# Clustered attention with an MLP behind it: loading and preparing the first keys and queries side by side, and queueing what later units need behind the first units

## The chip, the cores and the metric

The kernel runs on one core of a Trainium2 chip. The time is device microseconds (us) of one execution; the number given for the kernel before is the median of 3 runs. One further execution was profiled, and all durations below come from it.

## The reference

Four batches, 8 heads, 768 positions, head size 64, 16 cluster centres per head; then an MLP from 512 over 2048 back to 512 on all 3072 rows.

```python
q_assign = argmax(q_n . c_n); k_assign = argmax(k_n . c_n)        # nearest centre, per position
scores = where(q_assign == k_assign, (q . k) / 8, -1e9)
attn = softmax(scores);  x = attn . v                             # per batch and head
h = x @ w_in;  g = s * relu(h)**2 + b;  out = g @ w_out
```

## The kernel before

**Units.** The attention is cut into 192 units (`units`): a batch b, a pair of row tiles c (3 per batch), a pair of heads hp (4), a row tile t and a head h. Unit i takes 128 query rows of one head against all 768 keys. `scores` (L446, matmuls at L454) makes a 128x768 score tile in PSUM out of four matmuls: two with the transposed tiles KA and QA, two with KB and QB. `maxima` (L463) takes the row maximum on DVE, `exps` (L470 on DVE, L473 on ACT) the exponential `p`, `high` and `low` split p into two halves of 16 bits and turn them with a transposing DMA (L498), `values` (L502 on) multiplies by v. The first eight units (`RAW`) are done otherwise: p stays in 32 bits, PE turns it (L493), DVE and ACT copy the turned halves out of PSUM (L115, L117), and v is used as loaded. Score tiles have two PSUM buffers.

**Preparation.** `prep_k(b, hp)` makes KA and KB for a pair of heads: load `kn` (L78), row maximum on DVE (L97), maximum over the partitions by PE (`am_k`, L93, L94), a power-of-two scale `ksm` (L69 to L71, L65), a high half `ka` on ACT (L175), a low half `kb` on DVE (L177), a copy (L323), two transposing DMAs (L327, L328), matmuls with the centres (`pk`, L337, L338), a one-hot code of the nearest centre on DVE (`onehot`, L284 to L290) written into kb, and kb's transpose once more (L341). KB is complete only with that last DMA. `prep_q` does the same for the queries of four heads (loads `qn`; `qsm`; ACT L170, L171; POOL L173; DMAs L378 and L391). `prep_v` loads the four tiles `vn`, takes a common scale `vm` and splits each into `vh` (ACT L175) and `vl` (DVE L177). All three are generators: each `yield` is a place where the caller can turn to another one.

**Weights.** `weights` brings in w_in and w_out as 32 tiles of 512 KB, in turn; tile number p is `wst_p`, in a ring of three staging buffers (`stage`). `rebase` (ACT L193 and L195), `narrow` (DVE L199 and L200) and `bound` (PE L211 with DVE L212, or ACT L206; then POOL L213) turn one into the 32-bit tile `wi` or `wo`. A staging buffer is free when rebase and narrow of its tile are done. Three tiles are begun ahead of the units, and then one per unit.

**What sets the order.** All work is emitted as one Python sequence, and a scheduler at build time orders each engine's queue by priority and its own clock. On the chip every engine runs its queue strictly in order. All DMAs are issued by one queue (SP). `first_of_all` raises the priority of the first 20 units. In the kernel before, keys 0 and 1 and queries 0 are prepared in full one after the other, three weight tiles are begun, and `prepare(0)` to `prepare(3)` put keys 2 and 3, queries 1 and the first batch's v between the first units. Two small loads that spread the scalars s and b over 128 partitions (`sv`, `bv`, L121) are emitted before the keys.

The eight units that follow one load of queries need keys 0 (units 0 to 3) and keys 1 (units 4 to 7). Units 8 to 15 need keys 2 and 3 and queries 1. The MLP begins 21 units behind the attention and then takes a step per unit.

Of the kernel before, what the change touches and what calls it, by code (L numbers as in the profile page):

```python
# [2 lines left out]

# [11 lines left out]
ALU = mybir.AluOpType  # L15
# [11 lines left out]
def tile_cluster_attention_mlp(ctx, tc, q, k, v, cent, w_in, w_out, s_in, b_in, out):  # L27
# [44 lines left out]


    last_transpose = [None]

    def load(dst, src, free=False):
        if last_transpose[0] is None or free:
# [41 lines left out]
    def scalar_in(src, name):  # L119
        every = const([P, 1], F32, name)  # L120
        nc.sync.dma_start(every, src.partition_broadcast(P))  # L121
        return every


    ct = sb.tile([P, 2, D], F32, tag="r", name="ct", bufs=2)
    cn = ct[:, 0, :]
# [41 lines left out]
    def split(hi, lo, src, f, early):  # L168
        if early:
            A.activation(src, src, AF.Copy, scale=f)  # L170
            A.activation(hi, src, AF.Copy)  # L171
            yield
            G.tensor_tensor(lo, src, hi, op=ALU.subtract)  # L173
        else:
            A.activation(hi, src, AF.Copy, scale=f)  # L175
            yield
            V.scalar_tensor_tensor(lo, src, f, hi, op0=ALU.mult, op1=ALU.subtract)  # L177

# [119 lines left out]
    def prep_k(b, hp):  # L298
# [21 lines left out]
        else:  # L320
            ka = sb.tile([P, 2, T, 2, D], F16, tag="big", name=f"ka_{n}", bufs=BIGN)
        yield from split(ka[:, :, :, 0, :], kb[:, :, :, 0, :], kn, sm[2], False)
        V.tensor_copy(ka[:, :, :, 1, :], ka[:, :, :, 0, :])  # L323
        KA = sb.tile([P, 2 * T, P], F16, tag="KA", name=f"KA_{n}", bufs=5)
        KB = sb.tile([P, 2 * T, P], F16, tag="KB", name=f"KB_{n}", bufs=5)
        KS[(b, hp)] = (KA, KB)
        nc.sync.dma_start_transpose(KA, ka.rearrange("p h t e d -> p (h t e d)"))  # L327
        nc.sync.dma_start_transpose(KB, kb.rearrange("p h t e d -> p (h t e d)"))  # L328
        yield
        yield  # L330
        pa = (ps_m if b or not hp else ps_h).tile([P, 512], F32, tag="m" if b or not hp else "h", name=f"pk_{n}")
# [6 lines left out]
                nc.tensor.matmul(o, KB[:, i, :], cT[:, 2, hc], start=False, stop=True)  # L338
        mk = kb.rearrange("p h t e (r c) -> p (h t) e r c", c=C)[:, :, 1, :, :]
        yield from onehot(pa, 2 * T, f"k{n}", mk, BIG, -BIG)  # L340
        nc.sync.dma_start_transpose(KB, kb.rearrange("p h t e d -> p (h t e d)"))  # L341

    def prep_q(b, c, hq):
        n = f"{b}_{c}_{hq}"
# [53 lines left out]
    def prep_v(b):  # L398
        vm = sb.tile([P, 8], F32, tag="vm", name=f"vm_{b}", bufs=2)
        VM[b] = vm  # L400
        vns = []
        for hp in range(NP):
            vn = sb.tile([P, 2, T, D], F32, tag="kv", name=f"vn_{b}_{hp}", bufs=5)
            load(vn, v[b, 2 * hp : 2 * hp + 2].rearrange("h (p t) d -> p h t d", t=T), b == 0)
            vns.append(vn)
            if b == 0:
                VN[hp] = vn
            yield
        for hp in range(NP):
            absmax(vm[:, hp : hp + 1], vns[hp].rearrange("p h t d -> p (h t d)"))  # L410
            if hp < NP - 1:
                yield
        vc = columns(1, f"v{b}")
        V.tensor_reduce(vc, vm[:, 0:NP], axis=AX.X, op=ALU.max)
        if b:
            yield
        allmax(vm[:, 5:6], vc, f"v{b}")
        yield
        floor2(V, vm[:, 6:7], vm[:, 5:6])
        inverse2(V, vm[:, 7:8], vm[:, 6:7], 0)  # L420
        V.tensor_scalar(vm[:, 7:8], vm[:, 7:8], 2.0 ** 13, None, op0=ALU.mult)
        V.tensor_scalar(vm[:, 6:7], vm[:, 6:7], 2.0 ** -19, None, op0=ALU.mult)
        for hp in range(NP):
            vh = sb.tile([P, 2, T, D + 2], F16, tag="vh", name=f"vh_{b}_{hp}", bufs=5)
            vl = sb.tile([P, 2, T, D], F16, tag="vl", name=f"vl_{b}_{hp}", bufs=5)
            VS[(b, hp)] = (vh, vl)
            G.memset(vh[:, :, :, D:], 1.0)
            yield from split(vh[:, :, :, :D], vl, vns[hp], vm[:, 7:8], False)
            if hp < NP - 1:
                yield  # L430
                if b > 0:
                    yield
                    yield
# [11 lines left out]
    def scores(i):  # L445
# [5 lines left out]
        for X, Y, st in ((QA, KA, True), (QB, KB, False)):  # L451
            y = Y.rearrange("p n q -> p (n q)")
            for e in range(2):
                nc.tensor.matmul(  # L454
                    sc[:, e, :HALF], X[:, col, :], y[:, h * S + e * HALF : h * S + (e + 1) * HALF], start=st, stop=not st
                )
        U[i] = {"sc": sc[:, :, :HALF], "scale": qs[:, 3, hp % 2 : hp % 2 + 1]}

    def maxima(i):
        j = i % 4  # L460
        if j == 0:
            SM[i // 4] = sb.tile([P, 4, 4], F32, tag="ssm", name=f"ssm_{i}", bufs=4)
        V.tensor_reduce(SM[i // 4][:, 0, j : j + 1], U[i]["sc"], axis=AX.XY, op=ALU.max, negate=True)  # L463

    def exps(i):
        j = i % 4
# [3 lines left out]
        V.tensor_scalar(bi, sm[:, 0, j : j + 1], u["scale"], LIFT, op0=ALU.mult, op1=ALU.add)  # L470
        p = sb.tile([P, S], F32, tag="big", name=f"p_{i}", bufs=BIGN)
        total = {"accum_out": sm[:, 2, j : j + 1]} if i < RAW else {}
        A.activation(p.rearrange("p (a b) -> p a b", a=2), u["sc"], AF.Exp, bias=bi, scale=u["scale"], **total)  # L473
        u["p"] = p

    turned = ps_a.tile([P, CT, DM], F32, tag="acc", name="turned")
# [170 lines left out]
            nc.sync.dma_start(out[b * S : (b + 1) * S].rearrange("(p t) e -> p t e", t=T)[:, c * CT : (c + 1) * CT, :], o)  # L647


    sv = scalar_in(s_in, "sv")  # L650
    bv = scalar_in(b_in, "bv")
    steps = [(b, c, ft) for b in range(B) for c in range(NCH) for ft in range(NF)]
    NS = len(steps)
    active = []
# [29 lines left out]
    def run(gen):  # L684
        for _ in gen:
            pass

    def prepare(k):
        if k == 0:
            run(prep_k(0, 2))  # L690
            run(prep_k(0, 3))
            run(prep_q(0, 0, 1))
        if k == 1:
            for _ in range(5):
                next(first_v)
        if k == 3:
            next(first_v)
            next(first_v)
            active.append(first_v)

    first_v = prep_v(0)
    run(prep_k(0, 0))
    run(prep_k(0, 1))
    run(prep_q(0, 0, 0))
    for _ in range(3):
        next(wgen, None)
    i = 0
    while i < NU + 8 or i - LAG < NS + 4:
        m = i - LAG
# [61 lines left out]
```

## Time and profile before

| | |
|---|---|
| median of 3 runs | 1036.81 us (1032.09, 1036.81, 1037.48) |
| the profiled execution, whole | 1039.74 us |
| its span from first to last instruction | 1037.7 us |
| busy share of PE, DVE, ACT, POOL | 82%, 67%, 65%, 51% |
| mean busy share of the DMA queue's 16 engines | 75% |

The profile's page has five parts that matter here: busy time by engine, the span in 40 slices, the chain of work that ended last, groups of instructions, and DMA issues. The trace behind it answers by time: the instructions of one engine in order, with the idle time ahead of each and what ended it, or the busy time of every engine in chosen stretches. PE is the matmul engine, PEld its weight loads, DVE the vector engine, ACT the scalar engine, SPq the issue of DMAs by the SP queue. "PEclk" is the granted share of PE's clock. L12 is line 12 of the kernel before.

### The profile page before, as it was taken

The page shows a single profiled execution, that of the slowest core. Times are in us where ns is not written, and L with a number is a line of the kernel's source. Part 1 is how long each engine was busy: PE and PEld are TensorE (multiplying, and loading weights), DVE is VectorE, ACT ScalarE, POOL GpSimd, SP SyncE. Part 2 cuts the span into 40 slices and gives each one's busy share as a digit, 9 for nine tenths or more (in the row PEclk, how much of TensorE's full clock was granted, in tenths as well). Part 3 has the DMA queues.
Part 4 walks back from the last instruction along what each step waited for, and adds up shares of the span by engine and source line. Part 5 has one row for each costly group of instructions (what it writes and reads, how often), then busy time and mean ns, then how long its engine had stood idle before and what let it go on. Part 6 is the DMA issues. An engine that isn't in the chain of part 4 may idle for free.

```text
span 1037.7 us, 22320 instructions
## 1 busy us (share of the span) xinstructions
PE 855.8 (82%) x8536; PEld 588.5 (57%) x8536; DVE 692.8 (67%) x1690; ACT 679.5 (65%) x1232; POOL 527.7 (51%) x502
## 2 busy tenths in 40 slices
PE   0137766788888999988889898987788899999997
PEld 0125544555555677655557675655556676667764
DVE  6568688798798666777778755568767557674210
ACT  3136667668778778765668676655576677777543
POOL 2104465554467756554457565544455556666422
PEclk9998568999999999999889999999999899999999
DMA  8645689997687868799888978779896678877500
GB/s 237 155 91 143 154 208 209 201 218 139 128 154 138 153 117 138 149 196 156 183 159 154 168 126 160 142 136 197 154 171 118 142 124 163 136 125 134 81 27 21
DMA packets 473339, 153.16 MB, mean 148 GB/s; under 512 B 440976, under 2 KB 469648, under 8 KB 473232
## 3 DMA queue, kind: packets, MB, share of 16 engines
q1 hardware_dynamic: 473232, 151.73, 75.2%
q8 instruction: 67, 1.10, 0.4%
q14 instruction: 40, 0.33, 0.1%
HBM read 35.69 MB, written 6.29 MB: 40 GB/s over the span
## 4 chain that ended last, share of the span: by engine, by line
PE 40%; DVE 20%; DMA 14%; issue 6%; ACT 5%; POOL 4%; SPq 3%; POOLq 0%; DVEq 0%; ACTq 0%
PE h L591 14%; PE acc L635 13%; PE sc L454 6%; DVE ssm L463 4%; DMA kn<-in_k_dram 3%; POOL ph L496 3%; DMA KB<-kb 2%; DMA QB<-qb 2%; PE px L515 2%; DVE qa L177 2%; DMA wst<-in_moe_w_in_dram 2%; PE px L517 2%; PE px L516 2%; DMA qn<-in_q_dram 1%; ACT ph L483 1%
## 5 line engine op out<-in xcount | busy, mean ns | idle before, releaser
L496 POOL TENSOR_TENSOR ph<-p,ph 128x768 f16<-128x768 f32 x184 | 308.5, 1677 | 244.5 <-ACT ph L483 181.8
L635 PE MATMUL acc<-wos,g 128*128 128x512 f16 x1056 | 275.9, 383 | 6.0 <-POOL g L620 4.1
L591 PE MATMUL h<-x,wis 128*128 128x256 f16 x2112 | 269.3, 277 | 10.5 <-DMA x<-xn 6.2
L591 PEld LDWEIGHTS <-wis 128*128 128x128 f16 x2112 | 207.1, 99 | 63.8 <-issue 15.5
L473 ACT ACTIVATE p<-sc,ssm,qsm 128x768 f32<-128x768 f32 x192 | 188.2, 980 | 56.9 <-DVE ssm L470 30.5
L463 DVE TENSOR_REDUCE ssm<-sc 128x1 f32<-128x768 f32 x192 | 181.2, 950 | 50.0 <-PE sc L454 49.8
L620 POOL TENSOR_TENSOR g<-r,g 128x256 f16<-128x256 f32 x176 | 125.2, 713 | 111.2 <-ACT r L608 102.8
L483 ACT ACTIVATE ph<-p 128x768 f16<-128x768 f32 x184 | 153.3, 833 | 26.2 <-DMA PT<-ph 21.2
L601 ACT ACTIVATE r<-h,cf 128x256 f32<-128x256 f32 x176 | 82.2, 467 | 110.8 <-PE h L591 90.3
L515 PE MATMUL px<-vh,PT 128*128 128x65 f16 x1104 | 124.1, 199 | 23.7 <-DVE xs L529 7.1
L635 PEld LDWEIGHTS <-g 128*128 128x128 f16 x1056 | 95.2, 98 | 81.6 <-POOL g L620 7.9
L454 PE MATMUL sc<-KA,QA 128*128 128x384 f16 x384 | 101.0, 345 | 29.6 <-ACT p L473 17.4
L516 PE MATMUL px<-vl,PT 128*128 128x64 f16 x1104 | 124.4, 196 | 0.0
L517 PE MATMUL px<-vh,PT 128*128 128x65 f16 x1104 | 124.2, 197 | 0.0
L515 PEld LDWEIGHTS <-PT 128*128 128x128 f16 x1104 | 106.0, 100 | 29.3 <-issue 21.6
L516 PEld LDWEIGHTS <-PT 128*128 128x128 f16 x1104 | 106.0, 102 | 19.0 <-issue 10.8
L454 PE MATMUL sc<-KB,QB 128*128 128x384 f16 x384 | 101.1, 346 | 13.4 <-DMA QB<-qb 13.4
L517 PEld LDWEIGHTS <-PT 128*128 128x128 f16 x1104 | 106.1, 100 | 4.6 <-issue 1.1
L607 ACT ACTIVATE g<-r 128x256 f16<-128x256 f32 x176 | 72.8, 414 | 3.5
L608 ACT ACTIVATE r<-r 128x256 f32<-128x256 f32 x176 | 72.4, 412 | 3.5
L454 PEld LDWEIGHTS <-QA 128*128 128x128 f16 x384 | 35.3, 102 | 55.5 <-issue 25.2
L454 PEld LDWEIGHTS <-QB 128*128 128x128 f16 x384 | 38.4, 102 | 45.2 <-DMA QB<-qb 17.1
(165 smaller groups left out, 1161.0 us busy)
## 6 DMA issues: line engine op xcount, KB each, us to landing
wst<-in_moe_w_in_dram SPq DMA_DIRECT2D x16, 512.0 KB, 5.1
wst<-in_moe_w_out_dram SPq DMA_DIRECT2D x16, 512.0 KB, 4.5
kn<-in_k_dram SPq DMA_DIRECT2D x16, 384.0 KB, 3.8
vn<-in_v_dram SPq DMA_DIRECT2D x16, 384.0 KB, 4.0
qn<-in_q_dram SPq DMA_DIRECT2D x24, 256.0 KB, 3.7
out_dram<-o SPq DMA_DIRECT2D x12, 512.0 KB, 3.9
PT<-ph SPq DMA_TRANSPOSE x184, 4.0
x<-xn SPq DMA_TRANSPOSE x44, 2.9
```

Source lines behind the costliest of these rows:

```text
L454: nc.tensor.matmul(sc[:, e, :HALF], X[:, col, :], y[:, h * S + e * HALF : h * S + (e + 1) * HALF], start=st, stop=not st)
L463: V.tensor_reduce(SM[i // 4][:, 0, j : j + 1], U[i]["sc"], axis=AX.XY, op=ALU.max, negate=True)
L473: A.activation(p.rearrange("p (a b) -> p a b", a=2), u["sc"], AF.Exp, bias=bi, scale=u["scale"], **total)
L483: A.activation(u["ph"][:, 0, :], u["p"], AF.Copy)
L496: G.tensor_tensor(u["ph"][:, 1, :], u["p"], u["ph"][:, 0, :], op=ALU.subtract)
L515: nc.tensor.matmul(o1, PT[:, kt, :], vh[:, h, kt, : D + 1], start=(kt == 0), stop=False)
L516: nc.tensor.matmul(o, PT[:, kt, :], vl[:, h, kt, :], start=False, stop=False)
L517: nc.tensor.matmul(o1, PT[:, T + kt, :], vh[:, h, kt, : D + 1], start=False, stop=(kt == T - 1))
L591: nc.tensor.matmul(ph[:, :CW], WSP[ft][0][:, wl, kt, :], XS[(b, c, kt)][:, :, xl, :], start=(i == 0), stop=(i == len(terms) - 1))
L601: A.activation(r, ph[:, :CW], AF.Relu, scale=MS[(b, c)][0])
L620: G.tensor_tensor(g[:, 1, :], r, g[:, 0, :], op=ALU.subtract)
L635: nc.tensor.matmul(acc[:, t, :], g[:, gl, rows], WSP[ft][1][:, wl, :], start=(ft == 0 and gl + wl == 0), stop=(ft == NF - 1 and gl == 1))
```

## The change

The loads of keys 0, queries 0, keys 1, keys 2, keys 3 and queries 1 are emitted first, in this order, before any other work on them. Keys 0, queries 0 and keys 1 then go through their preparation in small steps in turn (`some(gen, n)` takes n steps). Keys 2, keys 3 and queries 1 (`second`) are taken two steps further at once, behind the first three's splits; their transposes come behind the last transpose of the first three; their centre matmuls and one-hot codes come after units 0, 1 and 2, one of them each.

The new helper `behind` puts each instruction emitted inside it behind a named instruction of the same engine, in the order alone (it adds no wait): behind the last split on DVE and ACT, the last transposing DMA on SP, the last score matmul, maximum and exponential. The loads of v, of s and b and of the weights are now emitted behind a transposing DMA, v in single steps between units 1 to 4.

```diff
+    last_turn = [None]
+    last_split = [None, None]
+    last_score = [None]
+    last_max = [None]
+    last_exp = [None]
...
+    def behind(*last):
+        stack = ExitStack()
+        for ins in last:
+            if ins is not None:
+                stack.enter_context(tc.issue_after(ins.ins))
+        return stack
...
-            load(vn, v[b, 2 * hp : 2 * hp + 2].rearrange("h (p t) d -> p h t d", t=T), b == 0)
+            load(vn, v[b, 2 * hp : 2 * hp + 2].rearrange("h (p t) d -> p h t d", t=T), False)
...
-    sv = scalar_in(s_in, "sv")
-    bv = scalar_in(b_in, "bv")
...
     def prepare(k):
         if k == 0:
-            run(prep_k(0, 2))
-            run(prep_k(0, 3))
-            run(prep_q(0, 0, 1))
-        if k == 1:
-            for _ in range(5):
-                next(first_v)
-        if k == 3:
-            next(first_v)
-            next(first_v)
-            active.append(first_v)
+            with behind(last_transpose[0]):
+                for gen in second:
+                    next(gen)
+        with behind(last_score[0], last_exp[0], last_max[0]):
+            if k == 1:
+                run(first_k[2])
+                some(first_v, 1)
+            if k == 2:
+                run(first_k[3])
+                some(first_v, 1)
+            if k == 3:
+                run(first_q[1])
+                some(first_v, 2)
+            if k == 4:
+                some(first_v, 1)
+                active.append(first_v)
 
     first_v = prep_v(0)
-    run(prep_k(0, 0))
-    run(prep_k(0, 1))
-    run(prep_q(0, 0, 0))
-    for _ in range(3):
-        next(wgen, None)
+    first_k = [prep_k(0, hp) for hp in range(NP)]
+    first_q = [prep_q(0, 0, hq) for hq in range(2)]
+    second = [first_k[2], first_k[3], first_q[1]]
+    for gen in (first_k[0], first_q[0], first_k[1], *second):
+        next(gen)
+    some(first_k[0], 2)
+    some(first_k[1], 2)
+    some(first_q[0], 2)
+    some(first_k[0], 1)
+    some(first_q[0], 1)
+    some(first_k[1], 1)
+    with behind(*last_split):
+        for _ in range(2):
+            for gen in second:
+                next(gen)
+    with behind(last_turn[0], *last_split):
+        some(first_v, 1)
+        sv = scalar_in(s_in, "sv")
+        bv = scalar_in(b_in, "bv")
+        some(wgen, 3)
+    run(first_k[0])
+    run(first_q[0])
+    run(first_k[1])
+    last_transpose[0] = last_turn[0]
```

The other lines record the instructions that `behind` names (`last_turn` at the transposes of KB, `last_split` at the high half and at L323's copy, and so on). No operation is added or removed; the amount of work is the same. In the changed kernel line numbers are 5 to 40 higher: L93 has become L98, L121 L126, L175 L187, L193 L205, L199 L211, L290 L302, L328 L340, L341 L353, L391 L403, L463 L475, L473 L485.

## What was predicted

> **What bounds the kernel now.** I read busy time by stretches first, then the queues of ACT, DVE and SP up to 101 us. The stretches, with the columns PE, PEld, DVE, ACT, POOL busy (and instructions), PE's clock, the DMA engines' busy share, GB/s:
>
> ```profile
> span 1037.7 us, 22320 instructions
> 0.00:47.90 47.90, 5.75 (x76) 3.50 (x77) 29.32 (x89) 14.57 (x26) 8.22 (x38) 1.00 0.75 195
> 47.90:70.20 22.30, 3.22 (x54) 1.78 (x52) 14.97 (x43) 5.67 (x10) 0.14 (x1) 1.00 0.57 116
> 70.20:95.40 25.20, 20.30 (x140) 15.79 (x141) 18.76 (x43) 15.84 (x33) 9.31 (x9) 0.93 0.52 129
> 95.40:100.80 5.40, 3.47 (x20) 2.38 (x20) 5.37 (x13) 4.19 (x10) 1.16 (x1) 0.72 0.59 191
> 100.80:160.00 59.20, 37.31 (x293) 26.22 (x291) 46.86 (x95) 37.71 (x64) 32.05 (x22) 0.64 0.74 166
> 160.00:240.00 80.00, 62.63 (x550) 42.51 (x551) 65.25 (x162) 56.97 (x102) 42.19 (x31) 0.96 0.97 207
> 240.00:1038.00 798.00, 723.13 (x7413) 496.29 (x7408) 512.29 (x1250) 544.52 (x994) 434.61 (x403) 0.97 0.75 139
> ```
>
> From 240 us on PE is busy 91% of the time (723 of 798): it is the bound. From 160 to 240 the DMA engines are at 97%. In the first 70 us nothing is full: PE works 9 us in all, and from 47.9 to 70.2 ACT 5.7 of 22.3 us. What holds the units there is seen in ACT's queue:
>
> ```profile
> 44.00 0.94 ACT L175 ACTIVATE ka<-kn,ksm 128x768 f16<-128x768 f32 x1 [5.95 <-DVE ksm L71]
> 56.16 0.93 ACT L175 ACTIVATE ka<-kn,ksm 128x768 f16<-128x768 f32 x1 [11.23 <-DVE ksm L71]
> 57.01 3.40 ACT L175 ACTIVATE vh<-vn,vm 128x768 f16<-128x768 f32 x4
> 68.77 0.91 ACT L170 ACTIVATE qn<-qn,qsm 128x256 f32<-128x256 f32 x2 [8.37 <-DVE qsm L361]
> 70.19 0.97 ACT L473 ACTIVATE p<-sc,ssm,qsm 128x768 f32<-128x768 f32 x1
> ...
> 100.79 1.01 ACT L473 ACTIVATE p<-sc,ssm,qsm 128x768 f32<-128x768 f32 x1
> ```
>
> and in DVE's:
>
> ```profile
> 7.59 0.95 DVE L97 TENSOR_REDUCE amb_k<-kn 128x1 bf16<-128x768 f32 x1 [2.93 <-DMA kn<-in_k_dram]
> ...
> 23.12 0.36 DVE L284 TENSOR_REDUCE om_k<-pk 128x12 f32<-128x192 f32 x1
> ...
> 43.61 0.29 DVE L290 TENSOR_SCALAR qb<-oo_q 128x512 f16<-128x512 f16 x1
> ...
> 47.93 1.82 DVE L463 TENSOR_REDUCE ssm<-sc 128x1 f32<-128x768 f32 x2 [1.68 <-PE sc L454]
> 49.67 0.33 DVE L470 TENSOR_SCALAR ssm<-ssm,qsm 128x1 f32<-128x1 f32 x2
> ...
> 95.37 0.94 DVE L463 TENSOR_REDUCE ssm<-sc 128x1 f32<-128x768 f32 x1
> ```
>
> Units 0 and 1 have maximum and bias at 50.0, but their exponentials come at 70.2: ACT stands in front of keys 3 (idle 11.2 us), v, and queries 1 (idle 8.4 us), which units 0 to 7 don't need. The exponential at 100.79 is unit 8's, the ninth. So the first unit costs 70.2 us, the next eight 30.6, and the other 183 the rest.
>
> **The change, part by part.** *ACT's queue.* Before, from the last weight operation ahead of unit 0 (`vh` is v's high half, `p_0` unit 0's exponential):
>
> ```order
> L206 ACTIVATE wo2_578,l1_131<-wo2_578 128x512
> L175 ACTIVATE ka_2_335<-kn_0_2_324,ksm_0_0_142 128x12x64
> L175 ACTIVATE ka_3_391<-kn_0_3_380,ksm_0_0_142 128x12x64
> L175 ACTIVATE vh_0_0_644<-vn_0_0_514,vm_0_513 128x12x64
> L175 ACTIVATE vh_0_1_727<-vn_0_1_516,vm_0_513 128x12x64
> L175 ACTIVATE vh_0_2_820<-vn_0_2_518,vm_0_513 128x12x64
> L175 ACTIVATE vh_0_3_909<-vn_0_3_520,vm_0_513 128x12x64
> L170 ACTIVATE qn_0_0_1_434<-qn_0_0_1_434,qsm_0_0_1_436 128x256 x2
> L171 ACTIVATE qb_0_0_1_450<-qn_0_0_1_434 128x4x64 x2
> L473 ACTIVATE p_0_496,ssm_0_493<-sc_0_488,ssm_0_493,qsm_0_0_0_253 128x768
> ```
>
> The changed kernel, same engine, same place:
>
> ```order
> L205 ACTIVATE wi1_273<-wst_2_274 128x512
> L218 ACTIVATE wo0_265,l1_131<-wo0_265 128x512
> L207 ACTIVATE wsg_2_417<-wst_2_274 128x512
> L485 ACTIVATE p_0_402,ssm_0_399<-sc_0_394,ssm_0_399,qsm_0_0_0_177 128x768
> L485 ACTIVATE p_1_463,ssm_0_399<-sc_1_456,ssm_0_399,qsm_0_0_0_177 128x768
> L485 ACTIVATE p_2_528,ssm_0_399<-sc_2_521,ssm_0_399,qsm_0_0_0_177 128x768
> L120 ACTIVATE PT_0_465<-turned_135 128x384
> L205 ACTIVATE wo1_413<-wst_3_414 128x512
> L207 ACTIVATE wsg_3_482<-wst_3_414 128x512
> L485 ACTIVATE p_3_591,ssm_0_399<-sc_3_584,ssm_0_399,qsm_0_0_0_177 128x768
> ```
>
> Keys 2, keys 3 and queries 1 went ahead of the weights, out of unit 0's way; v's halves went behind unit 6. But weight tile 3 now stands in front of unit 3, so that unit waits for a load.
>
> *SP's queue.* Before, around the last transposes for unit 0 (KB_0 and QB_0 complete with L341 and L391):
>
> ```order
> L78 DMA wst_4_546<-in_moe_w_in_dram 128x4x256
> L341 DMA_TRANSPOSE KB_0_0_157<-kb_133 128x12x128
> L78 DMA wst_5_579<-in_moe_w_out_dram 128x1024
> L341 DMA_TRANSPOSE KB_0_1_213<-kb_1_195 128x12x128
> L378 DMA_TRANSPOSE QA_0_0_0_275<-qa_0_0_0_266 128x8x128
> L391 DMA_TRANSPOSE QB_0_0_0_276<-qb_0_0_0_267 128x8x128
> ```
>
> The changed kernel:
>
> ```order
> L340 DMA_TRANSPOSE KB_0_1_211<-kb_1_140 128x12x128
> L83 DMA vn_0_0_256<-in_v_dram 128x2x384
> L126 DMA sv_258<-in_moe_s_dram 128x1
> L126 DMA bv_260<-in_moe_b_dram 128x1
> L83 DMA wst_0_263<-in_moe_w_in_dram 128x4x256
> L83 DMA wst_1_266<-in_moe_w_out_dram 128x1024
> L83 DMA wst_2_274<-in_moe_w_in_dram 128x4x256
> L353 DMA_TRANSPOSE KB_0_0_199<-kb_133 128x12x128
> L403 DMA_TRANSPOSE QB_0_0_0_206<-qb_0_0_0_191 128x8x128
> L353 DMA_TRANSPOSE KB_0_1_211<-kb_1_140 128x12x128
> ```
>
> The scalars and three weights moved from the head of the queue to just ahead of unit 0's last transposes; after these rows come five transposes for units 8 to 15 and only then `wst_3`.
>
> *First keys.* How fast the queue moves data:
>
> ```profile
> 2.00:4.00 2.00, 0.00 (x0) 0.00 (x0) 1.11 (x6) 0.28 (x2) 1.98 (x10) 1.00 0.06 6
> 4.00:6.00 2.00, 0.00 (x0) 0.00 (x0) 0.56 (x4) 0.00 (x0) 0.24 (x1) 1.00 0.34 45
> 6.00:8.00 2.00, 0.00 (x0) 0.00 (x0) 0.41 (x1) 0.00 (x0) 0.00 (x0) 1.00 1.02 371
> 18.00:22.00 4.00, 0.00 (x0) 0.00 (x0) 4.00 (x7) 1.28 (x3) 1.46 (x1) 1.00 1.12 224
> ```
>
> Three of SP's issues, and three kinds of DMA with size and median time to landing:
>
> ```profile
> 1.72 0.42 SPq L121 DMA_DIRECT2D bv<-in_moe_b_dram  x1
> 2.18 0.95 SPq L78 DMA_DIRECT2D kn<-in_k_dram  x2
> 43.97 1.23 SPq L391 DMA_TRANSPOSE QB<-qb  x1
> ```
>
> ```profile
> bv<-in_moe_b_dram SPq DMA_DIRECT2D x1, 0.5 KB, 4.7
> kn<-in_k_dram SPq DMA_DIRECT2D x16, 384.0 KB, 3.8
> wst<-in_moe_w_in_dram SPq DMA_DIRECT2D x16, 512.0 KB, 5.1
> ```
>
> DVE's groups up to 47.9 us (busy us, mean ns), and a rebase on ACT:
>
> ```profile
> L177 DVE SCALAR_TENSOR_TENSOR kb<-kn,ksm,ka 128x768 f16<-128x768 f32 x3 | 3.0, 1016 | 2.3 <-ACT ka L175 2.3
> L97 DVE TENSOR_REDUCE vm<-vn 128x1 f32<-128x768 f32 x3 | 2.8, 947 | 0.2 <-DMA vn<-in_v_dram 0.2
> L199 DVE TENSOR_SCALAR wi<-wi 128x512 int32<-128x512 int32 x3 | 1.3, 423 | 0.9 <-ACT wi L193 0.9
> L200 DVE SCALAR_TENSOR_TENSOR wi<-wst,wi 128x512 uint32<-128x512 uint32 x3 | 2.0, 679 | 0.0
> ```
>
> ```profile
> 96.61 0.66 ACT L193 ACTIVATE wi<-wst 128x512 f32<-128x512 f32 x1 [1.51 <-DMA wst<-in_moe_w_in_dram]
> ```
>
> From 2 to 6 us, behind the two scalar loads, almost nothing moves; then loads run at 371 GB/s. I book this 4 us stall on sv and bv, and it moves with them. Keys 0 then come at about 4.2 us in place of 7.6 (3.4 us). DVE's path to the one-hot codes gains the splits of keys 2 and 3, a reduction and small scale rows (about 5.4 us: twice 1.02, 0.7 for the reduction, some 2.7 in small rows at 0.17 and copies) and loses three weights' narrowing and one v reduction (4.3): the first one-hot row comes at 21 to 22.5, before 23.1. Keys 0 and queries 0 interleaved take 6 more: QB_0 can be issued at 28, before 43.97, where queries 0 came behind keys 1.
>
> *Unit 0.* KB_1's first transpose lands at about 23. Behind it v's tile and three weights, 0.39 + 3 x 0.52 = 1.97 MB at 371 GB/s, are 5.3 us, the scalars 4.0: 32.3. Only then KB_0 and QB_0, 0.39 + 0.26 MB at 224 GB/s (18 to 22 us: transposes alone), 2.9 us and about 0.8 to land: 36. Matmuls:
>
> ```profile
> 47.07 1.46 PE L454 MATMUL sc<-KB,QB 128*128 128x384 f16 x4 [4.35 <-DMA QB<-qb]
> ```
>
> The first two take 0.8: the maximum at 37 (before 47.9), then 1.8 and 0.3 on DVE: exponential 0 at 39 (before 70.2). Without the scalars' stall it would be 35.
>
> The Trainium skill (page "DMA: Bandwidth & Descriptors", section "Latency and other measured facts") gives transposing DMAs 261 GB/s; by that the transposes up to `wst_3`, 2.9 MB, would take 11.1 us in place of 12.9, and the forecast would be 2 us lower. The trace has 224, and I keep that.
>
> *Units 0 to 8.* 31 us earlier at unit 0 is not the gain, since postponed work now falls here. KB_1's second transpose, KA_2, KB_2, KA_3, KB_3 and QA_1 are 2.23 MB, 10 us after 35.2; `wst_3` is 1.4 more and lands at 47.5, so unit 3 comes at 49. On DVE the order holds nearly the same work before unit 0's maximum as before (keys 2, 3 and queries 1 against weights 3 to 5 and v), and so the same after it: 14.97 + 18.76 = 33.7 us from there to unit 8's maximum, which before took 47.5 us. From 37 it ends at 71 if DVE never waits, at 80 with the share of 70.2 to 100.8 us (24.13 of 30.6, 79%), at 85 with the 71% of the whole stretch. I take 79%, since waits on loads and on ACT stay, and 3 us from there to the exponential (before 5.4): unit 8 at 83, before 100.8, gain 18. Bounds: 73 and 95.
>
> *From unit 8 on* the queues hold the same operations in nearly the same order, and the weights stand at the same tile (10 and 11 ahead of unit 8's transpose). DMA has to move no more than before, and no wait there hangs on a time counted from the start. 18 us pass to the end: 1039.7 - 18 = 1021.7 for an execution like the profiled one. That lies 2.9 above the median, so I forecast 1036.8 - 18 = 1018.8, put as 1019. The builder's later order differs in places; I give that 4 us either way.
>
> **The rivals.** (a) *All of it comes through*: DVE runs almost full and unit 8 comes at 73: gain 28, 1009. For it: DVE's 5.37 of 5.40 us just before unit 8. Against: unit 3 behind a load.
>
> (b) *PE's clock*. The sparse units keep PE at half clock:
>
> ```profile
> 77.36 0.49 PE L454 MATMUL sc<-KB,QB 128*128 128x384 f16 x2
> ```
>
> Four score matmuls took 1.46 us at 47 us, two took 0.49 at 77: the early ones run at about two thirds of the rate or less, though the clock column has 1.00 there; from 100.8 to 160 it has 0.64. If all of units 0 to 8 ran at half, their 23.8 us of PE work (at 0.89 on average) would be 42.3, 18.5 more; the 6.8 us that PE was idle there hide some, 11.7 stay: unit 8 at 95, gain 6, 1031. Against: it was sparse before too. The Trainium skill (page "TensorE: Matmul & The Clock Gate", section "Part 1: The HAM clock gate") says that the array is throttled by default and that activity releases it, which speaks against spreading units thinner; the two rows agree with it.
>
> (c) *No change*: gain under 5.2 us, unit 8 at 96 or later, with DVE and ACT waiting in turn; 1035.
>
> (d) *Slower*: weight tiles 3 to 9 come one per round trip. Each stands on ACT in front of an exponential, and its buffer is free only behind rebase and narrow: 5.1 us to land, twice 0.65 on ACT, 0.42 + 0.68 on DVE, 7.5. Six after `wst_3`: 47.5 + 45 = 92.5, two one-hot transposes in SP's queue between them (1.8 each), then about 12 of ACT's queue to unit 8 (v's halves 3.4, an exponential, copies, six weight operations, tile 10's landing): 108, 7 later than before, 1044. It decides (5.2 us later, unit 8 at 106) from 7.2 us a tile on, and needs the ring of three to work as one. Against: tiles 3 to 5 are issued together.
>
> **How the numbers follow.** Forecast 0.58 (unit 8 at 77 to 91, 1013 to 1027), (a) 0.15, (b) 0.12, (c) 0.09, (d) 0.06. Within 0.5%, 5.2 us, a measurement can hardly tell from no change. Faster 0.85, same 0.09, slower 0.06. The range 1008 to 1032 takes in (a), the forecast and (b), and leaves out (c), (d) and a little of the edges.
>
> **What would show it.** Right: unit 0's exponential at 35 to 44, no keys or v ahead of it on ACT; idle time on ACT before unit 3 that ends with `wst`; the ninth exponential at 77 to 91; from there to the end about 937 us as before (1037.7 - 100.8). Wrong: unit 0 after 50 (then the scalars or the weights block QB_0), unit 8 after 96, or a tail longer by over 8 us.

## The result, and the profile after

The changed kernel takes 1013.65 us (median of 4 runs, 1006.12 to 1015.59), the kernel before 1037.14 (median of 4, 1032.09 to 1039.67): a ratio of 0.976 with a 95% interval of 0.972 to 0.980. It is faster by 23.5 us; 1019 were forecast. The profiled execution took 1015.59 us, with a span of 1013.5.

In the rows of the changed kernel L485 is the exponential, L475 the maximum, L205 a weight's rebase, L187 and L182 the high halves, L98 the matmul behind a tile's largest value. First rows of ACT's queue, with the start, the length, and in brackets the idle time ahead of it and what ended it:

```profile
32.09 0.66 ACT L205 ACTIVATE wi<-wst 128x512 f32<-128x512 f32 x1 [7.34 <-DMA wst<-in_moe_w_in_dram]
40.22 0.99 ACT L485 ACTIVATE p<-sc,ssm,qsm 128x768 f32<-128x768 f32 x1 [3.10 <-DVE ssm L482]
50.80 0.66 ACT L205 ACTIVATE wo<-wst 128x512 f32<-128x512 f32 x1 [3.75 <-DMA wst<-in_moe_w_out_dram]
51.92 0.98 ACT L485 ACTIVATE p<-sc,ssm,qsm 128x768 f32<-128x768 f32 x1
69.86 3.41 ACT L187 ACTIVATE vh<-vn,vm 128x768 f16<-128x768 f32 x4 [0.56 <-DVE vm L433]
80.14 0.98 ACT L485 ACTIVATE p<-sc,ssm,qsm 128x768 f32<-128x768 f32 x1
```

Unit 0's exponential comes at 40.22 (before 70.19), unit 3's at 51.92, unit 8's, the last row, at 80.14 (before 100.79). In the 15 us ahead of unit 0 ACT waits for no keys, v or queries any more; its waits are now for the first weight (7.34 us), for unit 0's own bias (3.10) and, ahead of unit 3, for weight 3 (3.75). Rows of DVE's queue over the same time:

```profile
4.34 0.95 DVE L102 TENSOR_REDUCE amb_k<-kn 128x1 bf16<-128x768 f32 x1 [0.36 <-DMA kn<-in_k_dram]
22.17 0.36 DVE L296 TENSOR_REDUCE om_k<-pk 128x12 f32<-128x192 f32 x1 [0.32 <-PE pk L350]
28.11 0.28 DVE L302 TENSOR_SCALAR qb<-oo_q 128x512 f16<-128x512 f16 x1
38.19 1.81 DVE L475 TENSOR_REDUCE ssm<-sc 128x1 f32<-128x768 f32 x2
75.85 0.94 DVE L475 TENSOR_REDUCE ssm<-sc 128x1 f32<-128x768 f32 x1
```

These are the first keys' reduction, the first row of one-hot codes, the one-hot codes of queries 0, unit 0's maximum and unit 8's. And busy time by stretches, with the columns PE, PEld, DVE, ACT, POOL, clock, DMA share, GB/s:

```profile
38.19:75.85 37.66, 27.91 (x190) 21.07 (x189) 32.49 (x80) 23.27 (x46) 5.02 (x5) 0.77 0.89 214
60.00:80.00 20.00, 15.09 (x87) 11.75 (x86) 19.24 (x50) 16.11 (x31) 6.96 (x7) 0.65 0.58 164
80.14:1013.50 933.36, 820.96 (x8250) 566.46 (x8248) 619.31 (x1505) 640.41 (x1158) 507.11 (x454) 0.96 0.78 147
```

From 60 to 80 us DVE is full (19.24 of 20). From unit 8 to the end it is 933.4 us, before 936.9.

**A ruler for the way to the end.** The builder gives every kernel another order of later work, so that "unit 100" is not the same amount of work in two kernels. I therefore count PE's work: in the trace I sum the moving columns of all matmuls in the order in which they end, fp32 ones four times (1,952,928 in every kernel here), and ask when a given share is done. The lead of the changed kernel over before by this ruler, in us:

| share of PE's work | 5% | 10% | 20% | 25% | 30% | 50% | 70% | 77.5% | 90% | 100% |
|---|---|---|---|---|---|---|---|---|---|---|
| before, us | 148.0 | 195.1 | 262.5 | 309.9 | 357.7 | 556.0 | 760.4 | 838.9 | 948.1 | 1032.4 |
| lead of the changed kernel | 23.2 | 21.8 | 23.7 | 24.8 | 15.7 | 17.8 | 18.5 | 25.1 | 24.1 | 24.1 |

The lead is made in the first 150 us, nine are lost between 25 and 30%, and seven come back between 70 and 77.5%. Each is about twice the 4 us that the forecast left for this.

### The profile page after: what moved, and what is told of

Read it like the earlier page. It is cut to its first block, busy times and chain, and to the rows that moved or that the text cites. A ratio compares the mean times of both kernels' runs of the same rounds, so it can differ in the third digit from the quotient of the medians.

```text
span 1013.5 us, 22310 instructions
## 1 busy us (share of the span) xinstructions
PE 859.0 (85%) x8536; PEld 593.8 (59%) x8536; DVE 681.9 (67%) x1690; ACT 680.6 (67%) x1232; POOL 526.8 (52%) x502
## 4 chain that ended last, share of the span: by engine, by line
PE 41%; DVE 16%; DMA 16%; ACT 8%; issue 7%; POOL 6%; SPq 2%; POOLq 0%; DVEq 0%; ACTq 0%
PE h L603 13%; PE acc L647 12%; PE sc L466 6%; DMA kn<-in_k_dram 4%; POOL ph L508 3%; DVE ssm L475 3%; ACT p L485 2%; DMA PT<-ph 2%; DMA QB<-qb 2%; DMA wst<-in_moe_w_in_dram 2%; ACT ph L495 2%; PE px L527 2%; PE px L529 2%; DMA qn<-in_q_dram 2%; PE px L528 2%
## 5 line engine op out<-in xcount | busy, mean ns | idle before, releaser
L485 ACT ACTIVATE p<-sc,ssm,qsm 128x768 f32<-128x768 f32 x192 | 188.2, 980 | 65.6 <-DVE ssm L482 29.1
L475 DVE TENSOR_REDUCE ssm<-sc 128x1 f32<-128x768 f32 x192 | 181.3, 950 | 33.2 <-PE sc L466 32.9
L466 PE MATMUL sc<-KA,QA 128*128 128x384 f16 x384 | 101.4, 345 | 23.8 <-ACT p L485 22.2
L527 PEld LDWEIGHTS <-PT 128*128 128x128 f16 x1104 | 105.4, 100 | 24.7 <-issue 16.7
L466 PE MATMUL sc<-KB,QB 128*128 128x384 f16 x384 | 100.3, 345 | 12.1 <-DMA QB<-qb 12.1
L535 DVE TENSOR_SCALAR ssm<-px 128x2 f32<-128x2 f32 x92 | 14.1, 153 | 78.1 <-PE px L529 77.8
L466 PEld LDWEIGHTS <-QA 128*128 128x128 f16 x384 | 36.0, 102 | 49.4 <-issue 27.9
```

What stands on the lines that cost most here:

```text
L466: last_score[0] = nc.tensor.matmul(sc[:, e, :HALF], X[:, col, :], y[:, h * S + e * HALF : h * S + (e + 1) * HALF], start=st, stop=not st)
L475: last_max[0] = V.tensor_reduce(SM[i // 4][:, 0, j : j + 1], U[i]["sc"], axis=AX.XY, op=ALU.max, negate=True)
L485: last_exp[0] = A.activation(p.rearrange("p (a b) -> p a b", a=2), u["sc"], AF.Exp, bias=bi, scale=u["scale"], **total)
L527: nc.tensor.matmul(o1, PT[:, kt, :], vh[:, h, kt, : D + 1], start=(kt == 0), stop=False)
```

## The experiments

Two theories of the start. **Start**: ACT's and SP's in-order queues held unit 0, and the new order of the first preparation frees it; the postponement shares out the rest. Its rivals are that the load order alone counts, or the postponement alone. Then, after the first four runs, two theories of the way to the end: **O**, that the builder's order of later work by itself is worth 5 us and far more, and **S**, that the start's gain passes one to one within 4 us.

### The new start without the postponement

```
     def prepare(k):
         if k == 0:
             with behind(last_transpose[0]):
                 for gen in second:
                     next(gen)
+            for gen in second:
+                run(gen)
-        with behind(last_score[0], last_exp[0], last_max[0]):
...
+        if k == 1:
+            some(first_v, 4)
+        if k == 3:
+            some(first_v, 2)
+            active.append(first_v)
```

> The changed kernel's new start (loads in lockstep, scalars and three weights behind unit 0's first transposes) without its postponement: the rest of keys 2, keys 3 and queries 1 and all of v are issued as before, ahead of unit 0 and in units 1 and 3, with nothing that holds them back. Theory (the in-order queues of ACT and SP kept unit 0 waiting, and the new start alone takes keys 2 and 3 out of its way on ACT): unit 0's exponential at 40 to 42 us; v's halves, again ahead of units 5 to 7 on ACT, cost the ninth exponential 2 to 6 us, 82 to 86; total 1014 to 1020. Rival 1 (only the load order counts): ninth exponential at 80, total 1013 to 1015, the same as the changed kernel. Rival 2 (only the postponement counts): unit 0 at 55 or later, ninth exponential at 95 or later, total 1030 or more.

Measured 1023.34 us, ratio 0.986 [0.983, 0.990]. Unit 0 at 39.86, unit 8 at 79.20, a little ahead of the changed kernel, though v's halves stand ahead of unit 6 (ACT's rows):

```profile
39.86 0.99 ACT L485 ACTIVATE p<-sc,ssm,qsm 128x768 f32<-128x768 f32 x1 [1.41 <-DVE ssm L482]
67.44 3.41 ACT L187 ACTIVATE vh<-vn,vm 128x768 f16<-128x768 f32 x4 [1.16 <-DVE vm L433]
79.20 0.98 ACT L485 ACTIVATE p<-sc,ssm,qsm 128x768 f32<-128x768 f32 x1
```

So the start alone brings the whole lead at unit 8, and the postponement adds nothing there. The total is 10 us worse than the changed kernel's all the same; its lead at a tenth of PE's work is 22.4, so these 10 us are lost later.

### The postponement without the new start

```
         if k == 0:
-            run(prep_k(0, 2))
-            run(prep_k(0, 3))
-            run(prep_q(0, 0, 1))
+            for gen in second:
+                next(gen)
+        with behind(last_score[0], last_exp[0], last_max[0]):
+            if k == 1:
+                run(second[0])
+                some(first_v, 2)
+            if k == 2:
+                run(second[1])
...
     for _ in range(3):
         next(wgen, None)
+    last_transpose[0] = last_turn[0]
```

Here `last_turn` is QB_0's second transpose.

> The kernel before with its old start (scalars first, keys 0, keys 1, queries 0 one after the other, three weights loaded between), and only the postponement: all of keys 2, keys 3 and queries 1 behind their loads is issued behind units 0, 1 and 2, v likewise, and later loads stand behind QB_0's transpose. Theory: unit 0's exponential comes as soon as its maximum, 44 to 50 us, but the work of keys 2, 3 and queries 1, which the old start did beside unit 0's own preparation, is now all behind it: some 42 us of DVE work at 79% from unit 0's maximum to unit 8's, the ninth exponential at 95 to 101, total 1031 to 1038. Rival 1 (only the load order counts): the same as before, 1037, with unit 0 at 65 or later. Rival 2 (only the postponement counts): ninth exponential near 83, total 1014 to 1020.

Measured 1030.57 us, ratio 0.993 [0.990, 0.995]. Unit 0 comes at 48.42, but units 2 and 3 at 69.53 and 84.35, and unit 8 at 106.33, later than before. ACT's rows (L484 is the exponential, L181 the queries' scaling):

```profile
48.42 0.99 ACT L484 ACTIVATE p<-sc,ssm,qsm 128x768 f32<-128x768 f32 x1 [17.49 <-DVE ssm L481]
68.71 0.92 ACT L186 ACTIVATE ka<-kn,ksm 128x768 f16<-128x768 f32 x1
69.53 0.97 ACT L484 ACTIVATE p<-sc,ssm,qsm 128x768 f32<-128x768 f32 x1
82.37 0.91 ACT L181 ACTIVATE qn<-qn,qsm 128x256 f32<-128x256 f32 x2 [1.89 <-DVE qsm L372]
84.35 0.97 ACT L484 ACTIVATE p<-sc,ssm,qsm 128x768 f32<-128x768 f32 x1
```

The wait moved from ahead of unit 0 to ahead of units 2 and 3: keys 3 still come 16 us behind keys 2 (52.5), queries 1 14 us behind keys 3. Its lead at a tenth is -1.1 us; the 6 us at the end come from later on.

### Only the loads in the new order

```
-    sv = scalar_in(s_in, "sv")
-    bv = scalar_in(b_in, "bv")
...
+    first = [prep_k(0, 0), prep_k(0, 1), prep_q(0, 0, 0)]
+    second = [prep_k(0, 2), prep_k(0, 3), prep_q(0, 0, 1)]
+    for gen in first + second:
+        next(gen)
+    sv = scalar_in(s_in, "sv")
+    bv = scalar_in(b_in, "bv")
-    run(prep_k(0, 0))
-    run(prep_k(0, 1))
-    run(prep_q(0, 0, 0))
+    for gen in first:
+        run(gen)
```

> The kernel before with the loads alone in the new order: six loads of keys and queries first, scalars and weights behind them; the preparation is issued in the old sequence, so ACT has keys 2, keys 3, v's halves and queries 1 ahead of unit 0 as before. Theory (ACT's in-order queue held unit 0): unit 0's exponential at 55 to 66 us, since v's halves and queries 1 still stand ahead of it and need loads and scales that come behind unit 0's transposes; ninth exponential at 88 to 97; total 1020 to 1034. Rival (load order alone): unit 0 at 45 or earlier, ninth exponential at 82, total 1016.

Measured 1046.91 us, ratio 1.011 [1.007, 1.015]: slower. Nothing that I expected of it came; ACT waits as before, to a tenth of a microsecond, for keys that have long been loaded (the first row is a weight's rebase):

```profile
14.67 0.66 ACT L193 ACTIVATE wi<-wst 128x512 f32<-128x512 f32 x1 [11.31 <-DMA wst<-in_moe_w_in_dram]
46.55 0.93 ACT L175 ACTIVATE ka<-kn,ksm 128x768 f16<-128x768 f32 x1 [5.97 <-DVE ksm L71]
58.65 0.93 ACT L175 ACTIVATE ka<-kn,ksm 128x768 f16<-128x768 f32 x1 [11.17 <-DVE ksm L71]
70.19 0.91 ACT L170 ACTIVATE qn<-qn,qsm 128x256 f32<-128x256 f32 x2 [7.31 <-DVE qsm L361]
71.62 0.97 ACT L473 ACTIVATE p<-sc,ssm,qsm 128x768 f32<-128x768 f32 x1
```

So load order alone is not the cause. For keys 0 and 1 the run is no clean test of it: ACT stands 11.31 us for the first weight ahead of their high halves, which come at 15.79 us in place of 12.74. But DVE has reduced keys 2, keys 3 and queries 1 by 12 us, and the waits for their scales are 5.97, 11.17 and 7.31 us, before 5.95, 11.23 and 8.37. Neither theory said what makes these scales late. It is in PE's rows of before. L93 is the matmul that spreads a tile's largest value; for keys 2, keys 3 and queries 1 it stands at

```profile
42.44 0.29 PE L93 MATMUL am_k<-identb,amb_k 128*128 128x128 bf16 x1 [0.71 <-DVE oe_q L285]
53.28 0.29 PE L93 MATMUL am_k<-identb,amb_k 128*128 128x128 bf16 x1 [0.85 <-DVE oe_k L285]
66.50 0.39 PE L93 MATMUL am_q<-identb,amb_q 128*128 128x128 bf16 x2 [0.85 <-DVE oe_k L285]
```

Each waits for the one-hot step (L285) of the tile in front of it, which reads the same PSUM bank: `h` has one buffer, and both the largest value and the code scores go through it. So the tiles form a chain: largest value, scale, split on ACT, two transposes, code scores, one-hot, and only then the next tile's largest value, 11 to 13 us a link (42.4, 53.3, 66.5). In PE's queue, too, each of the three stands right behind the code-score matmuls of the tile in front, and at the bank itself it waits for only 0.71 to 0.85 us; with a second buffer and the same order it would come earlier by that and no more, an estimate from these rows. The changed kernel takes all largest values before any code scores:

```profile
15.54 0.29 PE L98 MATMUL am_k<-identb,amb_k 128*128 128x128 bf16 x1 [4.69 <-DVE amb_k L102]
17.91 0.27 PE L98 MATMUL am_k<-identb,amb_k 128*128 128x128 bf16 x1 [2.08 <-DVE ksm L99]
18.55 0.37 PE L98 MATMUL am_q<-identb,amb_q 128*128 128x128 bf16 x2 [0.38 <-DVE ksm L71]
```

The three are there by 19 us. That the chain is the cause is read from these rows and from the loads' run; no run changes the bank alone or PE's order alone, so which of the two would be enough is not shown.

### The scalar loads in a gap

```
     for gen in (first_k[0], first_q[0], first_k[1], *second):
         next(gen)
+    sv = scalar_in(s_in, "sv")
+    bv = scalar_in(b_in, "bv")
...
         some(first_v, 1)
-        sv = scalar_in(s_in, "sv")
-        bv = scalar_in(b_in, "bv")
         some(wgen, 3)
```

> The changed kernel with the two scalar loads moved from ahead of the weights to right behind the first six loads, where the DMA engines of the changed kernel move almost nothing (11 and 0 GB/s from 10 to 14 us). Theory (the scalars stall the queue for 3 to 4 us wherever other transfers stand behind them): the stretch from 26 to 30 us, 63 and 173 GB/s in the changed kernel, fills up, QB_0 lands 3 us earlier, unit 0's exponential comes at 36 to 38 in place of 40.2, the ninth at 77 to 79; total 1009 to 1013. Rival (the thin stretch is the transposes' own, not the scalars'): exponential 0 at 40, total 1013 to 1015.

Measured 1033.34 us, ratio 0.993 [0.990, 0.996]. The start did what the theory says: unit 0 at 36.7 and unit 8 at 76.5, both 3.6 us earlier. Two stretches of the changed kernel (the last two columns are the DMA share and GB/s), and SP's issues of KB_0's first and second transpose in it:

```profile
26.00:28.00 2.00, 0.79 (x24) 0.73 (x24) 2.00 (x11) 0.00 (x0) 0.00 (x0) 1.00 0.22 63
28.00:30.00 2.00, 0.00 (x0) 0.00 (x0) 1.01 (x4) 0.00 (x0) 0.00 (x0) 1.00 0.65 173
```

```profile
13.01 1.51 SPq L340 DMA_TRANSPOSE KB<-kb  x1
27.13 6.37 SPq L353 DMA_TRANSPOSE KB<-kb  x1
```

The same of this kernel:

```profile
26.00:28.00 2.00, 0.36 (x14) 0.27 (x10) 1.77 (x8) 0.00 (x0) 0.00 (x0) 1.00 1.05 331
28.00:30.00 2.00, 0.00 (x0) 0.00 (x0) 0.90 (x3) 1.37 (x3) 0.00 (x0) 1.00 1.01 328
```

```profile
12.08 1.53 SPq L340 DMA_TRANSPOSE KB<-kb  x1
26.24 3.81 SPq L353 DMA_TRANSPOSE KB<-kb  x1
```

The issue of KB_0's transpose takes 2.6 us less and the thin stretch is gone. The other 0.9 us are there already at KB_0's first transpose, ahead of the place that the scalars left, and so are not theirs. So the two loads of 0.5 KB each cost 2.6 us where transfers stand behind them, and here nothing that can be seen; with the batches early (below) it is the same 2.6 us, 6.86 for 4.22. But the total is 20 us worse than the changed kernel's: a lead of 19.0 us at a tenth of PE's work shrinks to 13.4 at 30%, 4.5 at half, 4.0 at the end. The total's forecast (1009 to 1013) failed altogether, and with it "the lead passes one to one".

### The first weights behind unit 0's transposes

```
     with behind(last_turn[0], *last_split):
         some(first_v, 1)
         sv = scalar_in(s_in, "sv")
         bv = scalar_in(b_in, "bv")
-        some(wgen, 3)
...
     last_transpose[0] = last_turn[0]
+    some(wgen, 3)
```

> The changed kernel with its first three weight tiles behind unit 0's last transposes in place of ahead of them. Theory (unit 0 waits for QB_0 behind 1.97 MB of loads, but unit 8 waits for DVE's work and the weights' landing): unit 0's exponential at 33 to 36, 5 to 7 us earlier; the weights' work then falls between the units, and the ninth exponential comes at 77 to 81; total 1010 to 1015. Rival 1 (what unit 0 gains passes through): ninth exponential at 74, total 1007. Rival 2 (the weights' ring of three is a chain that sets unit 8): everything behind the weights is 5 us later, ninth exponential at 85, total 1018 or more.

Measured 1025.23 us, ratio 0.987 [0.984, 0.989]. Unit 0 at 34.33, 5.9 earlier, unit 8 at 80.72: what unit 0 gains is gone by unit 8, as expected. DVE is busy for 41.2 us between the two exponentials, in the changed kernel for 34.7, and unit 8's scores wait until 74.10 for queries 1's transpose. The lead at a tenth is 25.3, and 6 of it are gone at the end of the profiled execution. Again the total missed by 10 us.

### v's preparation behind unit 10

```
             if k == 3:
                 run(first_q[1])
-                some(first_v, 2)
-            if k == 4:
                 some(first_v, 1)
-                active.append(first_v)
+            if k == 11:
+                run(first_v)
```

> The changed kernel with v's three further reductions, its scales, its high halves (ACT) and low halves (DVE) put behind unit 10 in place of ahead of unit 8; v's loads stay. Theory (from unit 0's maximum to unit 8's DVE is the bound: 19.24 us busy of 20 from 60 to 80 us in the changed kernel): DVE loses 2.8 + 4.1 us there, so the ninth exponential comes 5 to 8 us earlier, at 72 to 75. The work is then done a few units later, so the lead over before at a tenth of PE's work stays 20 to 25 us; total 1005 to 1020 (builder's later order included). Rival (loads and transposes set unit 8, DVE only fills the wait): ninth exponential at 78 to 80.

Measured 1012.09 us, ratio 0.977 [0.973, 0.980], no different from the changed kernel. Unit 7's exponential comes 7 us earlier (67.97, there 74.97), unit 8's only 1.6. That is outside what I expected (72 to 75) and inside the rival's 78 to 80. Rows of all engines between the two:

```profile
67.97 0.98 ACT L485 ACTIVATE p<-sc,ssm,qsm 128x768 f32<-128x768 f32 x1
68.24 0.28 DVE L302 TENSOR_SCALAR qb<-oo_q 128x512 f16<-128x512 f16 x1
68.56 1.60 SPq L403 DMA_TRANSPOSE QB<-qb  x1
73.52 1.49 PE L466 MATMUL sc<-KB,QB 128*128 128x384 f16 x4
74.33 1.57 DVE L212 SCALAR_TENSOR_TENSOR wi<-wst,wi 128x512 uint32<-128x512 uint32 x1
75.83 1.81 DVE L475 TENSOR_REDUCE ssm<-sc 128x1 f32<-128x768 f32 x2
78.52 0.99 ACT L485 ACTIVATE p<-sc,ssm,qsm 128x768 f32<-128x768 f32 x1 [2.31 <-DVE ssm L482]
```

Unit 7's bias on DVE (L482), the scores of unit 8 (L466) in the changed kernel, and unit 7's bias in this one:

```profile
66.98 0.20 DVE L482 TENSOR_SCALAR ssm<-ssm,qsm 128x1 f32<-128x1 f32 x1
73.21 0.50 PE L466 MATMUL sc<-KB,QB 128*128 128x384 f16 x2 [0.18 <-DMA QB<-qb]
```

```profile
64.51 0.20 DVE L482 TENSOR_SCALAR ssm<-ssm,qsm 128x1 f32<-128x1 f32 x1
```

Of unit 7's 7 us, 2.5 are DVE's. The rest is ACT's queue: in the changed kernel the exponential comes 7.8 us behind its bias, with v's high halves (3.41 us) in front of it, here 3.3 us. Unit 8 waits for the next thing in line: queries 1's transpose is issued at 68.56, behind a weight and another load in the queue, and unit 8's scores come at 73.52, in the changed kernel at 73.21; a weight's 1.57 us on DVE comes between the scores and the maximum, which stands at 75.83 in place of 75.85. From 60 to 80 us DVE is busy for 19.24 of 20 us here too. So a full DVE there does not say that its work sets unit 8. The postponed work then costs the units behind: the lead at a tenth is 18.5.

### Another order of later work, the same start

The edit, in both kernels, touches only batches 1 to 3:

```
-                at(48 * b - 20 + 4 * hp, prep_k(b, hp))
-            at(48 * b - 20, prep_v(b))
+                at(48 * b - 21 + 4 * hp, prep_k(b, hp))
+            at(48 * b - 21, prep_v(b))
```

and with 19 in place of 21 for the later one.

> The kernel before, with one edit that has nothing to do with the start: keys and v of batches 1 to 3 are begun one unit earlier (21 units ahead of their batch in place of 20). The program's order is the same as before's up to unit 28 and differs from there to the end. Theory O (the builder's later order by itself moves the end by 5 to 15 us either way): a time off 1037 by 5 us or more, in either direction. Rival S (what the start gives reaches the end one to one, and the later order is worth 4 us at most): 1033 to 1041.

> The changed kernel with the same edit (keys and v of batches 1 to 3 one unit earlier). Up to unit 28 its order is the changed kernel's, so its lead over before at a tenth of PE's work is 20 to 25 us by either theory. Theory O: a time off 1014 by 5 us or more, and a distance to the kernel before with the same edit anywhere from 10 to 35 us. Rival S: 1010 to 1018, and a distance of 20 to 28 us.

> The kernel before with keys and v of batches 1 to 3 begun one unit later (19 units ahead). Order the same up to unit 28. Theory O: off 1037 by 5 us or more. Rival S: 1033 to 1041.

> The changed kernel with keys and v of batches 1 to 3 begun one unit later. Lead at a tenth of PE's work 20 to 25 us by either theory. Theory O: off 1014 by 5 us or more, distance to the kernel before with the same edit anywhere from 10 to 35 us. Rival S: 1010 to 1018, distance 20 to 28 us.

The same edit with 21 was put on the two kernels whose totals had missed most:

> The kernel with the scalar loads in the gap (1033 us in the first runs, though its units 0 to 8 led the changed kernel by 3.5 us), with keys and v of batches 1 to 3 begun one unit earlier, which gives another order from about unit 28 on. Theory O (its loss of 20 us against the changed kernel is the later order's): a time off 1033 by 5 us or more, 1008 to 1027, with the same lead of 19 to 24 us at a tenth of PE's work. Rival (something in its start costs the 20 us): 1028 to 1038 again.

> The kernel with the first weights behind unit 0's transposes (1025 us in the first runs, with a lead of 25 us at a tenth of PE's work), with keys and v of batches 1 to 3 begun one unit earlier. Theory O: a time off 1025 by 4 us or more, either way. Rival (its start costs 11 us against the changed kernel): 1021 to 1029 again.

All kernels together, with unit 0's and unit 8's exponential and the lead over before at a tenth of PE's work from the profiled executions, and the medians against those of before in the same runs (1036.76 to 1037.14):

| kernel | unit 0 | unit 8 | lead at a tenth | median | gain | ratio, interval |
|---|---|---|---|---|---|---|
| changed | 40.2 | 80.1 | 21.8 | 1013.65 | 23.5 | 0.976 [0.972, 0.980] |
| new start only | 39.9 | 79.2 | 22.4 | 1023.34 | 13.4 | 0.986 [0.983, 0.990] |
| postponement only | 48.4 | 106.3 | -1.1 | 1030.57 | 6.2 | 0.993 [0.990, 0.995] |
| loads only | 71.6 | 102.9 | -1.6 | 1046.91 | -10.1 | 1.011 [1.007, 1.015] |
| scalars in the gap | 36.7 | 76.5 | 19.0 | 1033.34 | 3.4 | 0.993 [0.990, 0.996] |
| the same, batches early | 37.0 | 76.8 | 20.7 | 1019.64 | 17.2 | 0.983 [0.979, 0.986] |
| weights behind | 34.3 | 80.7 | 25.3 | 1025.23 | 11.5 | 0.987 [0.984, 0.989] |
| the same, batches early | 34.4 | 80.9 | 25.5 | 1018.33 | 18.5 | 0.982 [0.979, 0.986] |
| v behind unit 10 | 39.1 | 78.5 | 18.5 | 1012.09 | 24.7 | 0.977 [0.973, 0.980] |
| before, batches early | 70.2 | 99.2 | 2.0 | 1037.11 | -0.1 | 1.001 [0.998, 1.003] |
| changed, batches early | 39.9 | 80.3 | 22.9 | 1013.92 | 23.1 | 0.977 [0.973, 0.980] |
| before, batches late | 70.1 | 99.3 | 0.9 | 1055.65 | -18.7 | 1.016 [1.013, 1.020] |
| changed, batches late | 39.7 | 79.8 | 22.7 | 1024.05 | 12.9 | 0.988 [0.985, 0.992] |

Two things follow. Under one and the same rule for the later batches the changed kernel beats before by 23.5, 23.2 and 31.6 us: the start's gain is real and does not hang on one lucky order. At a tenth of PE's work, which all three builds of each kernel reach in one and the same order, the three pairs are 21.8, 20.9 and 21.8 us apart; the three builds of before differ by up to 2.0 there, so the mark resolves no less. And the later order by itself moves the end by much more than 4 us: the kernel before loses 18.7 us when the next batch is begun one unit later, with nothing changed up to unit 28, and the scalars' kernel wins 13.7 back when it is begun one earlier. In the table, gain less lead at a tenth goes from -19.6 to +7.3. S does not hold. O holds in its size, not each time: four of these six runs moved by 5 us or more (18.7, 10.4, 13.7 and 6.9), while before and the changed kernel with batches early moved by 0.1 and 0.3, as S had it. None of the twelve is measurably faster than the changed kernel: v behind unit 10 and the changed kernel with batches early cannot be told from it. The others have longer medians, though for the scalars' and the weights' kernel with batches early the intervals still touch its own.

## Why the prediction was right, step by step

**What held unit 0.** Right in the place, short in the cause. ACT stood in front of keys 3, v and queries 1, and with that gone unit 0 came 30 us earlier; the postponement alone, with the old start, brings 22 of these (unit 0 at 48.42). But it brings nothing at unit 8 (106.33), since there keys 3 and queries 1 come later still (68.71 and 82.37, before 56.16 and 68.77). I did not ask why the scales were late. By PE's rows each tile's largest value stands behind the code scores of the tile in front, in PE's order and in a bank with one buffer. The prediction came out right because the change breaks that chain too. Had it been only a new load order, the same argument would have promised a gain, and the run above shows none by a tenth of PE's work (-1.6 us) and 10 us lost at the end.

**First keys, codes.** Keys 0 were forecast ready at 4.2 us and are at 4.34; the first one-hot row at 21 to 22.5, and is at 22.17; QB_0's codes at 28, and are at 28.11. The scalars' stall moved along as said, 2.6 us in place of 4.

**Unit 0** was forecast at 39 and came at 40.22: the maximum 1.2 us late (38.19 for 37).

**Weight 3** was forecast to land at 47.5 and unit 3 to follow at 49; ACT took the weight at 50.80, unit 3 at 51.92. The place of the wait was right, its size 3 us short.

**Units 0 to 8.** This is the term of the start that was mis-sized. DVE's work between the two maxima was put at 33.7 us and is 32.49; I gave it 79% of the time, it had 86% (32.49 of 37.66). The stretch is 5 us shorter than forecast (37.7 for 43), and the exponential follows its maximum by 4.3 us in place of 3: unit 8 at 80.14 for 83, a lead of 20.65 for 18. That DVE's work sets this time is not shown: without v's work on it unit 8's maximum came at the same time (75.83), and what its scores waited for in both was queries 1's transpose, which I had not named. That the lead came near the forecast rests on a share of DVE's time taken over from before, not on a bound that the runs confirm, and is in part luck.

**From unit 8 on** the profiled execution took 933.4 us for 936.9, inside the 4 us that I allowed. That step is right in its result and wrong in its size: the order of later work was worth up to 18.7 us in these runs, and in the changed kernel 9 lost and 7 won back nearly cancel. That the total came within 5.4 us of the forecast is in this part luck. The stretch of the loss, 25 to 30% of PE's work, before and after:

```profile
309.90:357.70 47.80, 43.80 (x443) 28.96 (x440) 36.41 (x82) 38.62 (x71) 36.05 (x34) 1.00 0.86 155
```

```profile
285.10:342.00 56.90, 47.44 (x479) 29.17 (x476) 38.33 (x90) 40.66 (x69) 38.64 (x34) 0.97 0.83 141
```

For the same work PE is idle 9.5 us in place of 4.0, and its matmuls take 3.6 more. Between 70 and 77.5% it goes the other way; from 70 to 75% the two are

```profile
760.40:816.40 56.00, 48.34 (x516) 33.35 (x516) 36.84 (x92) 36.23 (x65) 32.21 (x29) 0.91 0.76 146
```

```profile
742.00:792.30 50.30, 45.51 (x499) 31.71 (x499) 35.53 (x89) 36.03 (x65) 32.00 (x30) 0.97 0.93 162
```

before idle 7.7 us of 56.0 at a clock of 0.91, after 4.8 of 50.3 at 0.97. Which moved instruction does it stays open: the order differs in many places by then, and no run pins one.

**The rivals.** (a), all of it through with unit 8 at 73, failed: unit 3 stood behind weight 3, and unit 8's scores came only at 73.21, with queries 1's transpose. (b), the clock: it was low (0.65 from 60 to 80 us), and unit 8 did not come at 95. Three executions with the same order up to unit 8 (the changed kernel with its batches early, as it is, and late) went from unit 0 to unit 8 at a clock of 0.70, 0.74 and 0.79, in 40.4, 39.9 and 40.1 us. No run has a full clock there, so what the low clock cost in all is not shown. The Trainium skill ("TensorE: Matmul & The Clock Gate", "Part 1: The HAM clock gate") says that the clock falls to half when the array has been idle for a window of some 3.4 us. The trace agrees with the length, since the clock changes at 45.6, 52.4, 59.3, 62.7, 72.9 and 76.3 us in the changed kernel, each a multiple of some 3.4 us from the next, but not with the idleness: PE and its weight loads are never idle for more than 2.0 us from 47 to 80 us, and with the scalars in the gap the clock stays at 0.50 from 52.2 to 117.1 us with no idle time above 2.7. (c) and (d) failed: the weights did not come one per 7.5 us, the longest wait for one behind weight 3 was 1.06 us up to unit 8.

## What to carry over

Ask of a late operand why it is late, back to the first event, before counting a reordered queue as the cure: here three waits on one engine were, by the rows, one chain of short steps behind long ones, through PE's order and a PSUM bank with a single buffer. The start that takes all the short steps first brought the gain, while earlier loads alone or postponed work alone brought none of it by a tenth of PE's work. Price a change to the start at a mark that is behind it and ahead of the noise (a tenth of PE's work), in several kernels, and keep that price apart from the end: where a scheduler orders the rest, the same start can end 10 to 19 us apart. And a busy engine is not yet the bound: taking v's work away brought unit 7 forward by 7 us and unit 8 by 1.6, since unit 8 waited for a transpose.

## What the runs showed of the hardware that I had not expected

Two loads of a scalar to all 128 partitions, 0.5 KB each, cost the transfers behind them 2.6 us, as much as 0.96 MB at the 371 GB/s of the loads; put where no transfer waits, no cost of theirs can be seen. DVE's busy time depends on what POOL does: up to 85 us, in the changed kernel and in those with the scalars in the gap and with v behind unit 10, a weight's second step (L212) takes 0.68 or 0.69 us, but 0.80 to 1.65 in the eight rows that start while a POOL operation is under way. And the clock can stay at half for 65 us while PE is busy for 48 of them. This is the kernel with the scalars in the gap:

```profile
52.20:117.10 64.90, 48.09 (x287) 36.03 (x288) 51.32 (x115) 40.21 (x70) 28.63 (x21) 0.50 0.67 158
```

From unit 0 to unit 8 a clock of 0.70 to 0.79 made no difference above half a microsecond. These are the changed kernel, and the same with batches early and late:

```profile
40.22:80.14 39.92, 30.72 (x204) 23.17 (x204) 34.65 (x85) 26.19 (x51) 9.31 (x8) 0.74 0.86 216
39.91:80.32 40.41, 31.07 (x204) 22.98 (x204) 34.52 (x86) 26.09 (x51) 9.35 (x8) 0.70 0.85 213
39.73:79.82 40.09, 30.16 (x204) 22.46 (x204) 35.03 (x86) 26.16 (x52) 9.36 (x8) 0.79 0.84 215
```
